# More x transposes on TensorE, earlier q and k transposes and a new step order in an attention and SwiGLU kernel

## The chip, the cores and the metric

The kernel runs on one core of one Trainium2 chip. The metric is the device time of that core in microseconds (us) for one execution. One execution of each kernel was also recorded by the hardware profiler; the page and the trace of a kernel come from that one execution, and the timed series has three to eleven executions.

## The reference

The reference computes attention in a sliding window and feeds it to a gated feed-forward block (FFN). Cut to what matters:

```python
# q, k, v: (8, 8, 576, 64) float32;  x: 4608 tokens of 512;  d_ff = 1536
scores = scale * np.matmul(q, k.transpose(0, 1, 3, 2))
mask = np.abs(pos[:, None] - pos[None, :]) <= 32
attn = softmax(np.where(mask, scores, -1e9))            # written out in the original
x = (attn @ v).transpose(0, 2, 1, 3).reshape(4608, 512)
g, val = x @ w_gate, x @ w_val
out = (g / (1 + np.exp(-g)) * val) @ w_out               # float32, 4608 x 512
```

## The kernel before

The tokens pass through the FFN in nine chunks of 512. Chunk 0 is done in a prologue. Each of the chunks 1 to 8 is a list of steps: two 128-wide units (u50, u51) and five groups of seven products (0P1 to 4P7, a Strassen-Winograd scheme in which x and weights are added before the products and sums are formed after), then FFN2 as seven larger products (F1 to F7). While FFN2 of one chunk runs, the attention of the next batch is woven in: score tiles (sc), exponentials (ex), masks (k), attention products (av) and norms (m, n). The letter after a slash is the engine of a step (D VectorE, G GpSimd, A ScalarE), and @ gives PSUM banks.

On each engine the steps stand in the order in which the program issues them. That holds for the queue of SyncE too, called SPq in the profile: it carries the output sends, the DMA transposes of x, q and k, and the shifts of v, each in program order, and a transfer that has to wait holds up all that stand behind it.

An FFN product needs x with the model dimension on partitions, so each pair of 64-token tiles has to be turned. Pairs that are "urgent" are turned on TensorE, the others by a DMA transpose:

```python
def turn_x(ms, pool, cast=None):
    ...
    if pool is None:
        nc.sync.dma_start_transpose(out=dst, in_=x16[0])
        return
    ...
    for n, x in enumerate(x16):
        for g in range(GS):
            nc.tensor.transpose(out=tp[:, n, g, :], in_=x[:, 128 * g:128 * g + 128],
                                identity=ident)
```

The q and k of a batch arrive as tokens through GpSimd's queue, one chunk ahead of their use, and are turned by DMA, five pieces of q and five of k per batch:

```python
def turn_qk(b, m):
    turn_tok(toks.pop(("q", b, m)), qT[b % 2], m, 0)
    turn_tok(toks.pop(("k", b, m)), kT[b % 2], m, 32)
```

And the part of the chunk that says when this happens, with two steps:

```python
URGENT = {1: (1, 2), 2: (1, 2), 3: (0, 1), 4: (1,), 5: (0,)}

def chunk(j, name, todo):
    b = j + 1
    if 2 < b < B:
        load_v(b, range(5))
    ...
    def norm_carried(i):
        pair_norm(pairs[i])
        pair_xt(pairs[i])                 # DMA transpose of the carried pair
        if i == len(pairs) - 1 and b < B:
            for m in range(5):
                turn_qk(b, m)             # ten transposes, all behind the norm
                if m == 3:
                    shift_v_dma(b)
    ...
    def norm(i):
        pair_norm(todo[i])
        if i not in urgent:
            pair_xt(todo[i])
```

"F6" is the third of FFN2's seven products to be issued, "Fc11" the addition that makes the first output block and sends it.

Of the kernel before, what the change touches and what calls it, by code (L numbers as in the profile page):

```python
# [132 lines left out]
def kernel(  # L133
# [12 lines left out]
    B, H, S, D = q.shape  # L146
# [647 lines left out]
    for u in range(FKS):  # L794
# [14 lines left out]
        if u == 10:  # L809
# [35 lines left out]

    ORDER = {
        "first": """
            u50g0@2 u50v0@3 T1/G av@4@5 u50g1 ld0 u50v1 T3/D n0 u50s T2/D u50m 0P1@1 W0 0s1 1P1@0 W1
            ld1 1s1 0P2@7 1P5@5 0P5@6 ld2 0c11 0P6 0p5 W2 1P6 T4/D ld3 1P2@3 2P1@4 0u2 1c11 0P7 0c22
            ld4 1p5 2P5@2 1u2 W3 0P3 1P7 ld5 2p5 0c12 2s1 1c22 1P3 0P4 2P6 3P1@7 0sc 0sd ld6 1c12 2u2  # L850
            W4 2P2@6 1P4 0hm ld7 3s1 2P7 ld8 1sc 2c22 3P6 1sd 3u2 4P1@3 2sc ld9 2P3 2c11 2P4 3P2@5
            1hm 3P5@1 2c12 3P7 4s1 3c11 S10/G S12/G S00/G S11/D 2sd 3p5 4P6 3c22 4P5@6 u51g0@0 S13/G
            u51g1 2hm S20/G S02/D 4u2 4P7 4p5 3P4 4c22 3sc 4P2@2 4P4 u51s 3sd S22/D 3P3 S01/D S03/G
            4P3 4c11 3c12 4sc 4sd u51v0@7 4c12 tabE S21/G 3hm 4h1 S30/G u51v1 4h0 u51m S31/D sc0@4@5
            sc12@0@1@2@3 S40/D ex0 F1a@6 F1 S50/D ex2 S41/D k2 Fs1 S51/G k0 F2@7 ex1 S42/G F6 k1 W5
            S32/G Fc11 av012@4@5@0@1@2@3 Fu2 m0 F5 Fk5 sc34@4@5 m1 ex3 m2 S52/G S43/G S53/G tabS
            S23/D S33/D F7 xtp@2@3 Fc22 F3 W6 xtc/A k3 F4 Fc21 Fc12
        """,
        "even": """
            u50v0@3 u50g0@2 T3/D av@4@5 T1/G u50g1 u50v1 n0 u50s u50m 1P1@6 T2/G 0P1@0 1P5@7 1s1  # L860
            1P2@4 0P2@1 1P6 ld0 0s1 1c11 0P5@5 2P1@3 0c11 0P6 1p5 ld1 1u2 0p5 1P7 3P1@2 0u2 2s1 1c22
            2P5@4 T4/D 0P7 1P3 3s1 0c22 1P4 1c12 0P3 ld2 1sc 1sd 0c12 0P4 0sc ld3 ld4 1hm 2P6 2P2@7
            3P2@1 0sd 3P6 ld5 2p5 4P1@0 0hm 2c11 2u2 3u2 ld6 2P7 4s1 3P5@6 3P7 3c11 S12/G 3p5 2c22
            4P6 3c22 2P3 2P4 2c12 4P5@5 S00/G 2sc 4u2 3P4 S10/D S02/G 2sd S11/D 4P7 4p5 2hm S01/G
            4c22 ld7 3P3 3c12 u51g0@1 3sd 3sc u51g1 4P4 ld8 3hm S32/D 4sc 4P2@6 S03/G 4P3 u51s S30/G
            4sd S20/D u51v0@7 4c11 u51v1 4c12 tabE S22/G u51m ld9 S31/D sc12@0@1@2@3 sc0@4@5 ex2 4h0
            ex0 S50/G 4h1 F1a@6 F1 S21/D S40/D S51/G S23/D k2 F2@7 S41/G Fs1 k0 ex1 k1 S52/G Fc11
            S33/D S13/D S42/D F6 av012@4@5@0@1@2@3 Fu2 F5 m0 S53/D m1 Fk5 m2 F7 sc34@4@5@0@1 S43/D
            ex4 xtp@2@3 F3 Fc22 xtc/D F4 ex3 k4 tabS Fc12 Fc21 k3
        """,  # L870
        "odd": """
            T3/D u50g0@2 u50v0@3 T1/G av@4@5@0@1 u50g1 T2/G n0 u50v1 ld0 u50s u50m n1 0P1@7 1P1@6
            T4/G 1P2@4 0P5@5 0s1 1P5@2 ld1 1s1 1P6 1u2 0P2@3 0P6 4P1@0 1p5 1P7 2P1@1 0u2 1P3 1c11
            0c11 1c22 0p5 1c12 0P7 1P4 2s1 2P6 1sc ld2 ld3 1sd 0c22 ld4 1hm ld5 0P3 2P5@4 0sc 3P1@3
            ld6 2u2 2P2@2 2p5 0c12 0P4 2P3 3s1 2c11 S10/D 4s1 2P7 3P6 3P5@6 0sd 4P6 3P2@5 S11/D 2c12
            2c22 3u2 S13/G 3P7 2P4 3p5 0hm 4u2 3c11 4P5@2 2sc 2sd 3c22 2hm 4P7 4p5 ld7 4c22 3P4 3sc
            S12/G ld8 3P3 u51g0@7 u51g1 3sd 3c12 4P4 3hm 4P3 4sc S00/D 4c12 4P2@6 4c11 u51v0@4 S22/G
            u51s u51v1 4sd u51m 4h0 S50/D 4h1 S51/D S02/G S30/D sc12@0@1@2@3 S20/G S40/D S31/D F1a@6
            tabE ex1 S01/G F1 S21/G ld9 k1 sc0@4@5 ex2 k2 Fs1 S32/D F2@7 S41/G ex0 F6 S33/G k0 Fc11
            S52/D S43/D S42/D Fu2 av012@4@5@0@1@2@3 F5 Fk5 S53/D S23/D S03/D m0 F7 sc34@4@5 m2 F3 m1  # L880
            Fc22 ex3 xtp@2@3 F4 k3 tabS xtc/D Fc21 Fc12
        """,
        "seven": """
            u50g0@2 u50v0@3 av@4@5@0@1 u50v1 u50g1 u50s n0 n1 T1/G u50m 1P1@6 0P1@7 2P1@5 1s1 0s1
# [20 lines left out]
    def table(func):  # L905
        nc.scalar.activation(out=dummy, in_=rall[0:1, 0, 0:1], func=func, bias=0.0, scale=1.0)

    URGENT = {1: (1, 2), 2: (1, 2), 3: (0, 1), 4: (1,), 5: (0,)}

    def chunk(j, name, todo):  # L910

        nonlocal one, two
        b = j + 1
        if 2 < b < B:
            load_v(b, range(5))
        hts[j] = htpool.tile([128, FKS, 512], FP16, tag="ht", name="hT")
        xs, xsteps = x_sums(j)
        pairs = list(carried)
        carried[:] = todo[3:]
        n = len(todo)  # L920
        urgent = URGENT.get(j, ())
        loads = [(m, c) for m in range(5) for c in "qk"] if b + 1 < B else []
        engines = {"P": nc.tensor, "A": cast_act, "D": nc.vector, "G": nc.gpsimd}
        ex, turned = {}, []

        def av(i, pool=None):
            if i < n:
                pair_av(todo[i], pool, False)

        def attention():  # L930
            for i, m in enumerate(pairs):
                pair_av(m, (two[2], two[0])[i], False)

        def norm_carried(i):
            pair_norm(pairs[i])
            pair_xt(pairs[i])
            if i == len(pairs) - 1 and b < B:
                for m in range(5):
                    turn_qk(b, m)
                    if m == 3:  # L940
                        shift_v_dma(b)

        def scores(ids):
            for i in ids:
                if i < n:
                    ex[i] = pair_scores(todo[i], two[(2, 0, 1, 2, 0)[i]], False)
# [6 lines that stand above are left out]
        def load():  # L953
            if loads:
                m, c = loads.pop(0)
                load_qk(b + 1, (m,), c)

        steps = {"av": attention, "sc0": lambda: scores((0,)), "sc12": lambda: scores((1, 2)),
                 "sc34": lambda: scores((3, 4)),
                 "av012": lambda: [av(i, two[(2, 0, 1)[i]]) for i in range(3)],  # L960
                 "tabE": lambda: table(AF.Exp), "tabS": lambda: table(AF.Silu),
                 "xtp": lambda: turned.append(turn_x([todo[i] for i in urgent], two[1]))
                 if urgent else None,
                 "xtc": lambda eng: turned.pop()(cast_act if eng is cast_act else cast_dve)
                 if urgent else None,
                 "check": lambda: good.append(check_range()), "flag": lambda: set_flag(good[0], one[5])}
        for i in range(2):
            steps[f"n{i}"] = lambda i=i: norm_carried(i)
        for i in range(5):
            steps[f"ex{i}"] = lambda i=i: ex[i]()  # L970
            steps[f"k{i}"] = lambda i=i: pair_mask(todo[i])
            steps[f"m{i}"] = lambda i=i: norm(i)
        for i in range(10):
            steps[f"ld{i}"] = load
        for i in range(7):
            steps[f"W{i}"] = tw[i + 1]
        steps.update(xsteps)
        for f in range(5):
            for s, fn in group_steps(j, f, xs).items():
                steps[f"{f}{s}"] = fn  # L980
        for c in range(2):
            for s, fn in unit_steps(j, FKS - 2 + c, None if c or j == NCH - 1 else two[1]).items():
                steps[f"u5{c}{s}"] = fn
        for p in range(6):
            for k in range(4):
                steps[f"S{p}{k}"] = lambda eng, p=p, k=k: wino_sum(j, p, k, eng)

        stage = 0 if two else 1
        for token in ORDER[name].split():
            step, _, eng = token.partition("/")  # L990
            step, *banks = step.split("@")
            if stage == 0 and banks and step[:3] != "av" and step[:3] != "u50":
                one, two = open_psum(*[(f"ps_{i}", 1) for i in range(8)]), None
                stage = 1
            elif stage == 1 and todo and step in ("sc0", "sc12", "F1a"):
                two = open_psum(*[(f"ps_{i}", 1) for i in ("01", "23", "45", "6", "7")])
                stage = 2
            if step == "F1a":
                steps.update(wino_steps(j, j == NCH - 1, one if j == NCH - 1 else
                                        two[3:] if todo else one[6:]))  # L1000
            if eng:
                steps[step](engines[eng])
            elif stage == 1 and banks and step[0] != "F":
                steps[step](one[int(banks[0])])
            else:
                steps[step]()
# [42 lines left out]
```

## Time and profile before

| Before | |
|---|---|
| time, median of 3 runs | 337.9 us (335.4 to 338.69) |
| the recorded execution | 333.11 us, its records span 331.4 us |
| mean granted TensorE clock in it | 0.988 |
| TensorE busy | 303.4 us, 92% of the span |
| idle of TensorE in chunks 1 to 6 | 13.7 us |

The lines that name the waits are shown in the prediction. Read them as follows: in the list of waits, the line before the arrow is what stood still and the one after it what it waited for, then the total, the number and the longest wait. In the table of stretches, each row is a part of the span, and after its length comes the busy time of TensorE, its weight loads, VectorE, ScalarE and GpSimd, each with its count in brackets, then the granted clock, the DMA share and GB/s.

One more table shows the surroundings of the x wait at the end of chunk 4, in the same columns:

```profile
197.12:199.25 2.13, 0.00 (x0) 0.00 (x1) 0.37 (x2) 1.01 (x3) 0.00 (x0) 1.00 1.64 155
199.25:200.27 1.02, 1.02 (x6) 0.36 (x8) 0.00 (x0) 0.00 (x0) 0.94 (x1) 1.00 1.09 385
200.27:203.68 3.41, 3.41 (x41) 2.06 (x41) 0.90 (x2) 0.53 (x1) 3.32 (x4) 0.50 0.37 106
```

TensorE does nothing for 2.13 us; a microsecond after it resumed, its clock is granted at 0.50 for 3.41 us.

### The profile page before, as it was taken

The numbers are of one execution on the slowest core, as the hardware profiler recorded it, in microseconds if no ns is written. First come the engines' busy times: TensorE is split into PE (matmuls) and PEld (weight loads), VectorE is DVE, ScalarE is ACT, GpSimd is POOL, SyncE is SP. The second block draws the span as 40 slices with busy tenths as digits, with TensorE's granted clock in tenths as the row PEclk, the third lists the DMA queues.
The fourth block names the chain that finished last, engine by engine and source line by source line (L and its number), as shares of the span: only waits on it lengthen the run. The fifth ranks groups of instructions, "written<-read, shape, count | busy, mean of one in ns | idle before, by whom it ended". The sixth has DMA issues, their size and how long they took to land. (4 is left out here: it accounts for less than half of the span.)

```text
span 331.4 us, 8641 instructions
## 1 busy us (share of the span) xinstructions
PE 303.4 (92%) x3380; PEld 230.5 (70%) x3380; DVE 260.6 (79%) x501; ACT 217.7 (66%) x358; POOL 194.3 (59%) x245
## 2 busy tenths in 40 slices
PE   5789999898899998998999879989999999999991
PEld 2444555585678676886788666868787778878880
DVE  3845997798978996798869984898699978956970
ACT  3864569587468945796489653984699369529720
POOL 8972786926896683968576839477243333330440
PEclk9999999999999999999999997999999999999997
DMA  7999999999199999999999999999954250030012
GB/s 279 175 210 303 220 162 191 175 138 149 34 182 138 157 103 189 107 150 136 163 161 156 102 136 148 152 164 109 176 103 91 65 144 3 0 128 2 2 57 80
DMA packets 155920, 44.26 MB, mean 134 GB/s; under 512 B 136416, under 2 KB 153312, under 8 KB 155872
## 3 DMA queue, kind: packets, MB, share of 16 engines
q0 software_dynamic: 100640, 16.52, 71.6%
q1 hardware_dynamic: 55232, 27.11, 42.0%
q8 instruction: 28, 0.46, 0.6%
q14 instruction: 20, 0.16, 0.2%
HBM read 37.75 MB, written 9.44 MB: 142 GB/s over the span
## 5 line engine op out<-in xcount | busy, mean ns | idle before, releaser
L624 POOL TENSOR_TENSOR s_top<-hT 128x256 f16<-128x256 f16 x48 | 37.6, 800 | 57.2 <-DVE hT L535 42.7
L273 ACT ACTIVATE kept<-gX_ps 128x512 f32<-128x512 f32 x80 | 45.7, 598 | 11.5 <-PE gX_ps L509 9.2
L329 ACT ACTIVATE p_t<-s_ps 128x1024 f16<-128x1024 f32 (+1 forms) x40 | 35.8, 935 | 7.8 <-PE s_ps L323 7.6
L509 PEld LDWEIGHTS <-wv 128*128 128x128 f16 x320 | 31.6, 99 | 7.7 <-issue 2.6
L535 DVE TENSOR_TENSOR hT<-silu,val 128x1024 f16<-128x1024 f16 (+1 forms) x48 | 34.1, 724 | 1.2 <-ACT silu L531 0.4
L526 DVE TENSOR_TENSOR gate<-gX_ps,kept 128x512 f32<-128x512 f32 x40 | 27.5, 687 | 8.7 <-ACT kept L273 5.1
L521 DVE TENSOR_TENSOR val<-gY_ps,kept 128x512 f16<-128x512 f32 x40 | 26.9, 685 | 8.2 <-PE gY_ps L509 7.8
L653 PEld LDWEIGHTS <-s_top 128*128 128x128 f16 x288 | 27.3, 98 | 5.2 <-issue 0.8
L653 PEld LDWEIGHTS <-hT 128*128 128x128 f16 x288 | 27.1, 98 | 5.0 <-DVE hT L535 0.9
L509 PEld LDWEIGHTS <-g_top 128*128 128x128 f16 x288 | 28.2, 98 | 3.3
L228 POOL DMA_DIRECT2D tok<-in_k_dram x30 | 25.9, 864 | 7.2 <-DMA qT<-tok 6.8
L333 DVE TENSOR_TENSOR p_t<-p_t,mask 128x1024 f16<-128x1024 f16 x32 | 26.1, 843 | 4.3 <-ACT p_t L329 4.2
L509 PE MATMUL gX_ps<-x_sums,g_top 128*128 128x256 f16 x192 | 28.0, 273 | 0.0
L521 DVE TENSOR_TENSOR val<-gZ_ps,kept 128x512 f16<-128x512 f32 x40 | 27.2, 684 | 0.9 <-PE gZ_ps L509 0.4
L531 ACT ACTIVATE silu<-gate 128x512 f16<-128x512 f32 x40 | 25.1, 629 | 3.4 <-DVE gate L526 3.3
L509 PEld LDWEIGHTS <-g_more 128*128 128x128 f16 x256 | 25.1, 98 | 3.3
L228 POOL DMA_DIRECT2D tok<-in_q_dram x30 | 26.0, 867 | 1.9 <-DMA kT<-tok 1.1
L273 ACT ACTIVATE kept<-gZ_ps 128x512 f32<-128x512 f32 x40 | 23.9, 598 | 3.1 <-PE gZ_ps L509 2.9
L403 DVE TENSOR_TENSOR x<-o_ps,rall 128x512 f16<-128x512 f32 x36 | 24.9, 692 | 1.2
L531 ACT ACTIVATE silu<-gX_ps 128x512 f16<-128x512 f32 x40 | 23.9, 598 | 2.9 <-PE gX_ps L509 2.3
L509 PE MATMUL gX_ps<-x_sums,wg 128*128 128x256 f16 x160 | 24.0, 272 | 1.6 <-DVE gate L526 1.6
L624 POOL TENSOR_TENSOR s_top<-s_top,hT 128x256 f16<-128x256 f16 x23 | 18.9, 828 | 9.4 <-DVE s_top L624 9.1
(122 smaller groups left out, 689.8 us busy)
## 6 DMA issues: line engine op xcount, KB each, us to landing
out_dram<-osb SPq DMA_DIRECT2D x32, 256.0 KB, 3.9
v<-v SPq DMA_DIRECT2D x12, 264.0 KB, 5.6
v<-in_v_dram POOLq DMA_DIRECT2D x24, 128.0 KB, 5.7
tok<-in_q_dram POOLq DMA_DIRECT2D x24, 128.0 KB, 6.8
tok<-in_k_dram POOLq DMA_DIRECT2D x24, 128.0 KB, 6.7
qk_st<-in_q_dram SPq DMA_DIRECT2D x4, 576.0 KB, 7.0
qk_st<-in_k_dram SPq DMA_DIRECT2D x4, 576.0 KB, 8.8
v<-in_v_dram POOLq DMA_DIRECT2D x16, 96.0 KB, 5.4
```

Source lines behind the costliest of these rows:

```text
L228: nc.gpsimd.dma_start(out=t[0:n].rearrange("p (h d) -> p h d", d=D), in_=src[b].rearrange("h s d -> s h d")[128 * m:128 * m + n])
L273: nc.scalar.activation(out=o, in_=i, func=AF.Copy, bias=0.0, scale=1.0)
L329: nc.scalar.activation(out=o, in_=s, func=AF.Exp, bias=0.0, scale=1.0 / float(D) ** 0.5)
L333: nc.vector.tensor_tensor(out=flat, in0=flat, in1=mask, op=ALU.mult)
L403: nc.vector.tensor_tensor(out=x16s[m][:, a], in0=ov[:, :, :, 0:D], in1=r.unsqueeze(3).to_broadcast([128, a.stop - a.start, 4, D]), op=ALU. ...
L509: nc.tensor.matmul(out=k[name][:, n], lhsT=lhs[:, g, 128 * n:128 * n + 128], rhs=rhs[:, g, :], start=(pool is not None and n == 0 and g == 0),
L521: nc.vector.tensor_tensor(out=k["val"][:, :, cols(c)], in0=k[src], in1=k[name], op=ALU.add)
L526: nc.vector.tensor_tensor(out=k["gate"], in0=k["X"], in1=k["p5"], op=ALU.add)
L531: nc.scalar.activation(out=k["silu"][:, :, cols(c)], in_=k[src], func=AF.Silu, bias=0.0, scale=1.0)
L535: nc.vector.tensor_tensor(out=hts[j][:, 2 * f:2 * f + 2, c], in0=k["silu"][:, :, c], in1=k["val"][:, :, c], op=ALU.mult)
L624: eng.tensor_tensor(out=o, in0=a, in1=b, op=op)
L653: nc.tensor.matmul(out=dst[n], lhsT=lhs[:, f, 128 * n:128 * n + 128], rhs=rhs[:, f, :], start=(first and f == 0 and (split or n == 0)), st ...
```

## The change

The intent: all x that the next chunk needs at once is turned on TensorE, so that no DMA has to land in time; the q and k transposes start earlier, from FFN2 of the chunk before; and the order of steps in chunks 1 to 6 is replaced by one that is meant to tolerate small shifts. It has three parts, which I call X, T and O.

```diff
     ORDER = {
         "first": """   ... 10 lines replaced (part O) ...
         "even": """
 ... (the FFN2 part of it)
-            4sd S20/D u51v0@7 4c11 u51v1 4c12 tabE S22/G u51m ld9 S31/D sc12@0@1@2@3 sc0@4@5 ex2 4h0
-            ex0 S50/G 4h1 F1a@6 F1 S21/D S40/D S51/G S23/D k2 F2@7 S41/G Fs1 k0 ex1 k1 S52/G Fc11
-            S33/D S13/D S42/D F6 av012@4@5@0@1@2@3 Fu2 F5 m0 S53/D m1 Fk5 m2 F7 sc34@4@5@0@1 S43/D
-            ex4 xtp@2@3 F3 Fc22 xtc/D F4 ex3 k4 tabS Fc12 Fc21 k3
+            S11/G S21/D S30/G u51v1 4sd 4c11 tabE 4c12 u51m 4h0 4h1 sc12@0@1@2@3 S23/G ex1 F1a@6 ex2
+            S50/D S32/G S31/G S40/D F1 sc0@4@5 k1 S02/D F2@7 S41/G Fs1 ex0 k2 S13/D S51/G S52/D k0
+            S33/D F6 Fc11 av012@4@5@0@1@2@3 S43/D Fu2 S42/D m0 F5 m1 F7 m2 sc34@4@5@0@1 xtp@2@3 S03/D
+            Fk5 S53/D ex4 Fc22 F3 ex3 xtc/D tabS F4 k4 Fc12 k3 Fc21
         "odd": """     ... 10 lines replaced ...
-    URGENT = {1: (1, 2), 2: (1, 2), 3: (0, 1), 4: (1,), 5: (0,)}          # part X
+    URGENT = {1: (0, 1, 2), 2: (0, 1, 2), 3: (0, 1), 4: (0, 1), 5: (0,)}
+    turned_ahead = set()                                                  # part T, to the end
 ... in chunk(), at its top:
+        if b < B:
+            for m in range(4):
+                if (b, m) not in turned_ahead:
+                    turn_qk(b, m)
+            shift_v_dma(b)
 ... in norm_carried():
-                for m in range(5):
-                    turn_qk(b, m)
-                    if m == 3:
-                        shift_v_dma(b)
+                turn_qk(b, 4)
 ... in the loop over the steps:
+            if step == "F6" and b + 1 < B:
+                for m in range(2):
+                    turn_qk(b + 1, m)
+                    turned_ahead.add((b + 1, m))
```

In the old "even" order and in the new "odd" order, F6 stands behind Fc11, so that the early transposes of part T stand behind the first output's send in the queue. In the other new orders, F6 stands ahead of Fc11, and they stand ahead of the send. The x that the kernel before waits for is that of chunks 3 and 5, sent at the ends of chunks 2 and 4, which have the "even" order.

More of the change, by code (lines that the diff above doesn't have):

```diff
@@ L847 @@
         "first": """
-            u50g0@2 u50v0@3 T1/G av@4@5 u50g1 ld0 u50v1 T3/D n0 u50s T2/D u50m 0P1@1 W0 0s1 1P1@0 W1
-            ld1 1s1 0P2@7 1P5@5 0P5@6 ld2 0c11 0P6 0p5 W2 1P6 T4/D ld3 1P2@3 2P1@4 0u2 1c11 0P7 0c22
-            ld4 1p5 2P5@2 1u2 W3 0P3 1P7 ld5 2p5 0c12 2s1 1c22 1P3 0P4 2P6 3P1@7 0sc 0sd ld6 1c12 2u2
-            W4 2P2@6 1P4 0hm ld7 3s1 2P7 ld8 1sc 2c22 3P6 1sd 3u2 4P1@3 2sc ld9 2P3 2c11 2P4 3P2@5
-            1hm 3P5@1 2c12 3P7 4s1 3c11 S10/G S12/G S00/G S11/D 2sd 3p5 4P6 3c22 4P5@6 u51g0@0 S13/G
@@ L853 @@
-            u51g1 2hm S20/G S02/D 4u2 4P7 4p5 3P4 4c22 3sc 4P2@2 4P4 u51s 3sd S22/D 3P3 S01/D S03/G
-            4P3 4c11 3c12 4sc 4sd u51v0@7 4c12 tabE S21/G 3hm 4h1 S30/G u51v1 4h0 u51m S31/D sc0@4@5
-            sc12@0@1@2@3 S40/D ex0 F1a@6 F1 S50/D ex2 S41/D k2 Fs1 S51/G k0 F2@7 ex1 S42/G F6 k1 W5
-            S32/G Fc11 av012@4@5@0@1@2@3 Fu2 m0 F5 Fk5 sc34@4@5 m1 ex3 m2 S52/G S43/G S53/G tabS
-            S23/D S33/D F7 xtp@2@3 Fc22 F3 W6 xtc/A k3 F4 Fc21 Fc12
+            W0 W1 u50v0@3 u50g0@2 u50g1 av@4@5 u50v1 T1/G n0 u50s T2/D u50m 1P1@7 ld0 1P2@1 0P1@6
@@ new lines @@
+            0P5@0 1s1 T3/D 1P5@4 ld1 ld2 0s1 1P6 ld3 0P6 1u2 1c11 0P2@5 2P1@2 1p5 T4/D 1P7 W2 0c11
+            1P3 0u2 2s1 0P7 2P5@1 ld4 1c22 1c12 0p5 W3 1sc ld5 0P3 2p5 1P4 2P6 3P1@3 2P2@4 0c22 0P4
+            1sd 4P1@5 2u2 0sc 0c12 1hm 3s1 2P7 3P6 W4 2P3 S12/D 2c11 0sd 4s1 0hm 3u2 3P5@0 2c22 3P2@7
+            3P7 S00/D 4P6 2P4 ld6 ld7 3p5 2c12 3c22 3c11 2sc S01/G 4u2 4P5@1 3P4 2sd 4P7 3P3 S10/G
+            u51g0@4 2hm S20/G 4p5 3sc u51g1 4c22 3sd 3c12 4P4 3hm 4P3 S11/D 4P2@6 4sc S21/G u51v0@7
@@ L858 @@
+            S30/G 4c12 u51s 4c11 S03/G u51v1 u51m 4sd 4h0 sc0@4@5 ld8 sc12@0@1@2@3 tabE F1a@6 ld9 ex0
+            4h1 S23/D S50/D S40/D ex2 F1 S31/G Fs1 S51/D k0 F2@7 ex1 k2 S41/G S22/D F6 k1 Fc11 S52/G
+            av012@4@5@0@1@2@3 S32/G F5 S53/D S33/D S13/G m0 Fu2 sc34@4@5 S02/G m2 S42/G m1 Fk5 S43/D
+            ex3 W5 tabS F7 xtp@2@3 xtc/A Fc22 F3 W6 F4 k3 Fc12 Fc21
         """,
         "even": """
-            u50v0@3 u50g0@2 T3/D av@4@5 T1/G u50g1 u50v1 n0 u50s u50m 1P1@6 T2/G 0P1@0 1P5@7 1s1
@@ L861 @@
-            1P2@4 0P2@1 1P6 ld0 0s1 1c11 0P5@5 2P1@3 0c11 0P6 1p5 ld1 1u2 0p5 1P7 3P1@2 0u2 2s1 1c22
-            2P5@4 T4/D 0P7 1P3 3s1 0c22 1P4 1c12 0P3 ld2 1sc 1sd 0c12 0P4 0sc ld3 ld4 1hm 2P6 2P2@7
-            3P2@1 0sd 3P6 ld5 2p5 4P1@0 0hm 2c11 2u2 3u2 ld6 2P7 4s1 3P5@6 3P7 3c11 S12/G 3p5 2c22
-            4P6 3c22 2P3 2P4 2c12 4P5@5 S00/G 2sc 4u2 3P4 S10/D S02/G 2sd S11/D 4P7 4p5 2hm S01/G
-            4c22 ld7 3P3 3c12 u51g0@1 3sd 3sc u51g1 4P4 ld8 3hm S32/D 4sc 4P2@6 S03/G 4P3 u51s S30/G
@@ L866 @@
-            4sd S20/D u51v0@7 4c11 u51v1 4c12 tabE S22/G u51m ld9 S31/D sc12@0@1@2@3 sc0@4@5 ex2 4h0
-            ex0 S50/G 4h1 F1a@6 F1 S21/D S40/D S51/G S23/D k2 F2@7 S41/G Fs1 k0 ex1 k1 S52/G Fc11
-            S33/D S13/D S42/D F6 av012@4@5@0@1@2@3 Fu2 F5 m0 S53/D m1 Fk5 m2 F7 sc34@4@5@0@1 S43/D
-            ex4 xtp@2@3 F3 Fc22 xtc/D F4 ex3 k4 tabS Fc12 Fc21 k3
+            u50g0@2 u50v0@3 u50g1 T1/G av@4@5 u50v1 u50s n0 u50m 0P1@7 T2/G T3/G 1P1@0 0P5@1 1P2@6
+            1s1 1P5@4 0s1 0p5 1P6 1c11 0P2@5 0c11 1u2 0P6 1p5 3P1@2 1P7 0P3 ld0 0u2 ld1 T4/D 1c22
@@ new lines @@
+            2P1@3 0P7 0c12 2P5@6 1P4 1P3 ld2 2s1 2P6 1sc 4P1@5 0c22 2P2@1 ld3 0P4 0sc ld4 1c12 1sd
+            2u2 ld5 2P7 2p5 3s1 ld6 4s1 2P3 1hm 3P6 0sd 2c11 ld7 3u2 S10/D 2c22 4P6 2c12 2sc 0hm
+            3P5@0 3P2@4 3P7 2P4 3c11 3p5 4u2 3c22 4P5@6 2sd ld8 S00/G 4P7 3P4 4p5 S01/D 3sc 3P3 2hm
+            3sd 4c22 4sc u51g0@1 u51g1 S12/G 3c12 4P4 S20/G 4P2@7 4P3 u51v0@4 S22/D ld9 u51s 3hm
+            S11/G S21/D S30/G u51v1 4sd 4c11 tabE 4c12 u51m 4h0 4h1 sc12@0@1@2@3 S23/G ex1 F1a@6 ex2
+            S50/D S32/G S31/G S40/D F1 sc0@4@5 k1 S02/D F2@7 S41/G Fs1 ex0 k2 S13/D S51/G S52/D k0
@@ L870 @@
+            S33/D F6 Fc11 av012@4@5@0@1@2@3 S43/D Fu2 S42/D m0 F5 m1 F7 m2 sc34@4@5@0@1 xtp@2@3 S03/D
+            Fk5 S53/D ex4 Fc22 F3 ex3 xtc/D tabS F4 k4 Fc12 k3 Fc21
         """,
         "odd": """
-            T3/D u50g0@2 u50v0@3 T1/G av@4@5@0@1 u50g1 T2/G n0 u50v1 ld0 u50s u50m n1 0P1@7 1P1@6
-            T4/G 1P2@4 0P5@5 0s1 1P5@2 ld1 1s1 1P6 1u2 0P2@3 0P6 4P1@0 1p5 1P7 2P1@1 0u2 1P3 1c11
-            0c11 1c22 0p5 1c12 0P7 1P4 2s1 2P6 1sc ld2 ld3 1sd 0c22 ld4 1hm ld5 0P3 2P5@4 0sc 3P1@3
@@ L875 @@
-            ld6 2u2 2P2@2 2p5 0c12 0P4 2P3 3s1 2c11 S10/D 4s1 2P7 3P6 3P5@6 0sd 4P6 3P2@5 S11/D 2c12
-            2c22 3u2 S13/G 3P7 2P4 3p5 0hm 4u2 3c11 4P5@2 2sc 2sd 3c22 2hm 4P7 4p5 ld7 4c22 3P4 3sc
-            S12/G ld8 3P3 u51g0@7 u51g1 3sd 3c12 4P4 3hm 4P3 4sc S00/D 4c12 4P2@6 4c11 u51v0@4 S22/G
-            u51s u51v1 4sd u51m 4h0 S50/D 4h1 S51/D S02/G S30/D sc12@0@1@2@3 S20/G S40/D S31/D F1a@6
-            tabE ex1 S01/G F1 S21/G ld9 k1 sc0@4@5 ex2 k2 Fs1 S32/D F2@7 S41/G ex0 F6 S33/G k0 Fc11
@@ L880 @@
-            S52/D S43/D S42/D Fu2 av012@4@5@0@1@2@3 F5 Fk5 S53/D S23/D S03/D m0 F7 sc34@4@5 m2 F3 m1
-            Fc22 ex3 xtp@2@3 F4 k3 tabS xtc/D Fc21 Fc12
+            u50g0@2 T3/G T1/G u50v0@3 av@4@5@0@1 T2/G u50v1 ld0 n0 u50g1 u50s ld1 n1 u50m 0P1@7 0s1
+            0P2@6 1P5@4 1P1@0 ld2 ld3 1s1 0P6 2P1@3 0c11 1P2@6 0P5@5 1p5 T4/D 0u2 0p5 1P6 0P7 1u2
+            1c11 2P2@1 0c22 0P3 2s1 0c12 1P7 0sc 1c22 ld4 0P4 2P5@2 1P3 0sd 2P6 3P1@7 0hm 2p5 1sc 2u2
+            3s1 4P1@6 1P4 2P7 3P6 ld5 2P3 1c12 2c11 2c22 1sd 4s1 1hm 3P5@5 3u2 S00/G 4P6 3P7 S10/D
@@ new lines @@
+            2c12 S02/G S01/G 3p5 3P2@4 S12/G 2P4 2sc S03/G 4P5@1 3c22 4u2 3c11 2sd 4P7 ld6 3P4 S11/D
+            2hm 4p5 3P3 4c22 3sc u51g0@2 u51g1 ld7 4P4 4P2@0 3c12 3sd 3hm 4P3 u51v0@7 4sc S20/G ld8
+            S13/D 4c11 u51s 4c12 S30/D 4sd u51v1 4h1 tabE S21/G 4h0 S22/G u51m S40/D sc0@4@5 S50/D
+            ld9 sc12@0@1@2@3 S31/G F1a@6 F1 ex0 ex1 F2@7 Fs1 S51/G k0 S41/D k1 S43/D ex2 S23/D k2
+            Fc11 S42/D F6 S32/D S53/G av012@4@5@0@1@2@3 S52/D F5 m0 m1 sc34@4@5 Fu2 Fk5 S33/D m2 F7
@@ L882 @@
+            F3 xtp@2@3 ex3 tabS Fc22 k3 Fc12 F4 xtc/D Fc21
         """,
```

## The prediction

> **What bounds the kernel now.** I read the busy shares first, then TensorE's own list of waits, then stretches cut at the chunk borders, and last the timeline around the longest waits.
>
> ```profile
> PE 303.4 (92%) x3380; PEld 230.5 (70%) x3380; DVE 260.6 (79%) x501; ACT 217.7 (66%) x358; POOL 194.3 (59%) x245
> DMA  7999999999199999999999999999954250030012
> ```
>
> TensorE is busy 92% of 331.4 us, so it is the bound and can gain at most its idle 28 us. The row of digits says that the DMA engines are over 90% busy in nearly every slice of the first three quarters: a transfer there waits its turn. The list of TensorE's waits (total, times, longest) names who holds it up:
>
> ```profile
> PE gv_ps L583 <- DMA xT<-x: 3.6, 2, 2.1
> PE o_ps L385 <- DVE p_t L333: 2.7, 8, 0.6
> PE s_ps L323 <- DMA kT<-tok: 2.0, 2, 1.1
> PE gX_ps L509 <- DVE gate L526: 1.6, 2, 0.9
> PE s_ps L323 <- DVE val L521: 1.5, 3, 0.5
> PE gX_ps L509 <- DVE hT L594: 1.4, 1, 1.4
> PE y_ps L653 <- DVE osb L682: 0.8, 1, 0.8
> ```
>
> No single cause leads; it is a dozen short waits. Cut at the starts of chunks 1 to 6, the only ones whose order changes (the orders "seven" and "last" are the same text), the stretches are (window, length, busy of each engine, clock, DMA share, GB/s):
>
> ```profile
> 58.60:95.20 36.60, 32.29 (x378) 25.80 (x377) 31.91 (x59) 24.54 (x40) 25.02 (x31) 1.00 1.29 123
> 95.20:130.40 35.20, 32.50 (x395) 26.06 (x393) 29.71 (x56) 24.97 (x41) 22.43 (x28) 1.00 1.70 154
> 130.40:163.60 33.20, 32.18 (x393) 26.17 (x394) 27.55 (x57) 22.90 (x38) 24.55 (x28) 1.00 1.52 140
> 163.60:199.25 35.65, 32.24 (x390) 25.79 (x388) 29.99 (x57) 24.97 (x41) 22.70 (x28) 1.00 1.50 144
> 199.25:233.50 34.25, 33.15 (x388) 26.59 (x389) 26.83 (x57) 22.87 (x38) 24.33 (x28) 0.95 1.46 142
> 233.50:266.30 32.80, 31.65 (x387) 25.75 (x386) 28.32 (x53) 23.57 (x39) 11.92 (x15) 1.00 0.48 107
> ```
>
> Length less PE busy is the idle time: 4.3, 2.7, 1.0, 3.4, 1.1 and 1.2, together 13.7 us. This is all that the change can touch; prologue and last two chunks stay. In the timeline, the two largest kinds look so:
>
> ```profile
> 149.59 2.55 SPq L234 DMA_TRANSPOSE qT<-tok  x1
> 151.84 0.29 PE L323 MATMUL s_ps<-qT,kT 64*128 64x64 f16 x8 [0.90 <-DMA kT<-tok]
> 152.23 1.19 SPq L234 DMA_TRANSPOSE kT<-tok  x1
> 192.18 3.19 SPq L419 DMA_TRANSPOSE xT<-x  x2
> 199.25 0.61 PE L583 MATMUL gv_ps<-xT,wg 128*128 128x512 f16 x2 [2.13 <-DMA xT<-x]
> ```
>
> In odd chunks the ten q and k transposes, issued only after the carried pair's norm, are still in the queue when the scores need them. And x sent to DMA at 192.2 is first usable at 199.25, 7 us later, although the next chunk's first product needs it.
>
> **What the skill says.** "VectorE: DVE Perf Modes", section "The three transpose paths", gives 390 ns for a 128x128 transpose on TensorE and 1309 ns on the DMA path. The trace agrees in direction, but in chains: four on TensorE take 0.39 to 0.40 us together, eight 0.61; one x transpose (four blocks) by DMA holds its queue 1.2 us and lands after 4.6 us in the median. "DMA: Bandwidth & Descriptors", section "Issuing engines are not separate DMA queues", says transfers issued by different engines share the same 16 DMA engines and interleave. The 90% digits and the 7 us agree. "Perfetto Trace Analysis", section "Optimizing Scalar/DVE Operations", says that GpSimd and VectorE share an SBUF read port. It shows: an x sum on VectorE took 1.38 us beside GpSimd's at 58.3 us, against a usual 0.42; so who takes which sum matters. No page bears on the step order itself.
>
> **The change part by part.** The built programs differ by 12 TensorE transposes with their 12 weight loads; counts of products, exponentials and sums stay.
>
> (1) x turned on TensorE. Chunks 1, 2 and 4 turn one pair more, each with four matmuls. Two of these pairs are the ones awaited at 130.4 (1.43 us) and 199.25 (2.13 us). Removed: 3.56. Added on TensorE: eight against four costs 0.21, so 3 x 0.21 = 0.6. The evacuating copies grow by a pair too (0.41 to 0.69 on VectorE; 0.60 to 1.00 to 1.47 on ScalarE), but one or two FFN2 products of 1.3 us lie between transposes and the next chunk, so I count them as hidden. Net gain 2.9.
>
> (2) q and k transposes early. Four of ten now stand before the FFN2 sums' sends in the queue's program order, four at the chunk's top, two after the carried norm. One holds the queue 1.2 to 2.5 us, so four fewer after the norm end the series 5 us or more earlier, against waits of 0.90 and 1.10 (plus 0.1 of the same kind). Gain 2.0. They also free token buffers earlier; the wait of GpSimd for those (5 us once) has no cost on TensorE in the list.
>
> (3) The order. I followed each wait to its producer in both programs.
> - Chunk 1, first product: today it waits 1.41 for VectorE's hT of unit 50. The new first product goes to a bank that the last prologue eviction freed, and only the second waits for hT: four matmuls cover 0.43. VectorE has three w_top (0.55 each) ahead of it instead of one and the 1.38 sum: 1.65 against 1.93, another 0.28. Gain 0.7.
> - Chunk 1, gate waits (0.77 and 0.87): VectorE stood 1.38 us for a GpSimd sum that directly preceded its use. Now four VectorE steps, some 2.8 us, lie between that sum and its use. Gain 1.4.
> - Chunk 1, the second y product waits 0.84 for the first output's addition, which stood behind a 1.02 us weight sum. That moves away. Gain 0.7.
> - Even chunks: the first attention product waits 0.73 each time for the last mask (3 x 0.73 = 2.2), and the last score tile 0.53, 0.53 and 0.40 for a VectorE addition. The new order gives that tile's bank later and puts a sum and two products around it; but now the first FFN2 product waits for the same addition, with only the 0.87 us of two score tiles and unit 51 before it. I give it half: 1.8.
>
> Sum of (3): 4.6. All three: 2.9 + 2.0 + 4.6 = 9.5 us of the 13.7.
>
> **Less new waits.** Every order puts something new on an edge. I take 0.4 us for each of the six reordered chunks, 2.4 in all, an estimate from the size of the small waits in the list (0.2 to 0.6). Net: 9.5 - 2.4 = 7.1, so 337.9 - 7.1 = 330.8 us, 2.1% less.
>
> **Rivals.**
> First, a wait takes the place of the one removed. VectorE is busy 26.8 to 31.9 us in stretches of 33 to 37: when TensorE closes up, VectorE has less time for the same work. In odd chunks the k wait of 1 us now lets VectorE catch up before FFN2; without it FFN2's first product may wait for hT instead. For: the same chain (addition, hT, product) already costs 0.5 in even chunks. Against: odd chunks have 2 us less VectorE work than even ones. Then (2) gives nothing and (3) half: 2.9 + 2.3 - 1 = 4.2, or 333.7.
>
> Second, the early transposes collide. They enter a DMA system that is already full, beside token and v loads, and in odd chunks stand in the queue between the first output's send and the second's, where four of them need 5 to 6 us. An output buffer returning late would stop VectorE or ScalarE, and the v loads could land late. For: the 90% digits. Against: the work is the same, only moved, and outputs of the next chunk's gates come over 5 us later. It would eat (2) and some of (1): 334 to 335.
>
> Third, the gain is larger than the trace shows. The unprofiled runs took 335.4 to 338.7, the profiled 333.1. If the extra 2 to 6 us are waits that vary from run to run, an order with slack wins part of them too: 327. If they are clock throttling (two stretches of half clock in this trace, 0.988 in the mean), nothing is won. The trace can't tell.
>
> **Range and chances.** Between the second rival (335) and the third (327) lies my range: 327 to 335. The limit of 2% is 331.1, which is practically my point value: the chance of more than 2% faster is 0.50, within 2% 0.47. Slower than 344.7 would need new waits of over 16 us in six chunks: 0.03.
>
> **What would show it.** If right: TensorE's list has no wait on xT<-x and none on kT<-tok; L425 has 76 matmuls instead of 64; chunk 1 loses about 3 us, chunks 2 and 4 about 2 to 3 each, chunks 3 and 5 about 1; idle time in chunks 1 to 6 falls from 13.7 to about 6. If the first rival: waits on hT L535, val L521 or p_t L333 grow in the odd chunks. If the second: VectorE or ScalarE waiting for DMA on osb, or attention products waiting for v. The prediction is wrong if PE idle in chunks 1 to 6 falls by under 4 or over 11 us, or if the time moves without it, through the clock.

## The result and the profile after

The changed kernel takes 324.86 us in the median of 4 runs (324.24 to 325.4); the kernel before, with one more run beside it, takes 337.98 us (335.4 to 338.69). The ratio is 0.9624, with a 95% interval of 0.9571 to 0.9678, so it is 3.8% faster. Ratios here are the mean time of one kernel's fast runs over that of the other's in the same rounds, so they are not quite the ratio of the medians that I quote. On one core a run counts as slow if it is over 1.5% above the fastest of its kernel, and in the sessions of the experiments, one to four of the eleven widely spread runs of the kernel before are left out by that rule.

The time lies below my range (327 to 335), while the direction was right.

From the page of the changed kernel, first the busy shares, then the clock by slices:

```profile
PE 301.0 (93%) x3392; PEld 230.6 (71%) x3392; DVE 257.0 (80%) x498; ACT 217.0 (67%) x358; POOL 195.7 (61%) x248
PEclk9999999999999999999999999999999999999997
```

TensorE has twelve instructions more and is busy 2.4 us less: the row of the clock has no slice below 9 before the last, so the half-clock stretch within the kernel is gone. The list of TensorE's waits, same columns as before:

```profile
PE o_ps L385 <- DVE p_t L333: 3.8, 6, 1.5
...
PE gY_ps L509 <- DVE hT L594: 1.0, 1, 1.0
PE s_ps L323 <- DVE val L521: 0.7, 2, 0.4
```

In this list no line says xT<-x and none says kT<-tok: TensorE waits for no DMA in the reordered chunks. The waits for x (3.6 us) and for k (2.0 us) are not shortened, they are absent. One is new: attention products now wait 1.5 us for a mask in chunk 1. The stretches, cut at the starts of chunks 1 to 6:

```profile
59.26:93.88 34.62, 31.84 (x382) 26.11 (x381) 31.64 (x59) 24.64 (x40) 23.79 (x30) 1.00 1.40 143
93.88:126.98 33.10, 32.16 (x399) 26.23 (x397) 28.14 (x55) 24.01 (x39) 23.93 (x29) 1.00 1.60 153
126.98:159.80 32.82, 31.96 (x395) 26.31 (x393) 28.90 (x56) 23.63 (x41) 24.33 (x30) 1.00 1.41 126
159.80:192.96 33.16, 32.10 (x394) 26.02 (x392) 28.06 (x55) 23.90 (x39) 25.67 (x31) 1.00 1.84 165
192.96:225.54 32.58, 31.74 (x390) 26.09 (x388) 28.36 (x56) 23.79 (x41) 22.94 (x28) 1.00 1.52 133
225.54:258.27 32.73, 31.96 (x386) 25.42 (x384) 26.51 (x53) 23.20 (x39) 11.85 (x15) 1.00 0.71 111
```

The six lengths sum to 199.0 us against 207.7 before, 8.7 less. Length less busy time gives an idle of 7.3 us against 13.7, 6.4 less; the other 2.3 us are busy time that went away, 1.7 of it the half-clock stretch shown above. Chunk by chunk the trace lost 2.0, 2.1, 0.4, 2.5, 1.7 and 0.1 us. Prologue and the last two chunks changed by 0.7 us at most.

How the border from chunk 2 to chunk 3 looks now, in the timeline (start, duration, engine, line, operation):

```profile
109.36 1.84 SPq L234 DMA_TRANSPOSE kT<-tok  x1
...
123.68 0.84 PE L425 MATMUL xt_ps<-ident,x 128*128 128x128 f16 x12
...
126.98 0.59 PE L583 MATMUL gv_ps<-xT,wg 128*128 128x512 f16 x2
```

Three pairs are turned on TensorE in 0.84 us; the next chunk's first product starts with no wait in brackets behind it. And a k transpose for the scores of chunk 3 already runs at 109 us in chunk 2, before any output of this chunk is sent.

So, from one recorded execution to the other, the span fell from 331.4 to 323.1 us, by 8.3, which is near my 7.1. But the medians differ by 13.1. The recorded execution of the kernel before was 4.8 us below the median of its runs; that of the changed kernel (324.83 us) sits at its median. The experiments had to explain this second amount.

### The profile page after: what moved, and what is told of

Same layout as the page of the kernel before. It is cut to its first block, busy times and chain, and to the rows that moved or that the text cites. A ratio compares the mean times of both kernels' runs of the same rounds, so it can differ in the third digit from the quotient of the medians.

```text
span 323.1 us, 8668 instructions
## 1 busy us (share of the span) xinstructions
PE 301.0 (93%) x3392; PEld 230.6 (71%) x3392; DVE 257.0 (80%) x498; ACT 217.0 (67%) x358; POOL 195.7 (61%) x248
## 5 line engine op out<-in xcount | busy, mean ns | idle before, releaser
L624 POOL TENSOR_TENSOR s_top<-hT 128x256 f16<-128x256 f16 x43 | 30.7, 722 | 60.6 <-DVE hT L535 42.5
L535 DVE TENSOR_TENSOR hT<-silu,val 128x1024 f16<-128x1024 f16 (+1 forms) x48 | 32.8, 695 | 1.9 <-ACT silu L531 1.2
L624 POOL TENSOR_TENSOR s_top<-s_top,hT 128x256 f16<-128x256 f16 x30 | 23.9, 802 | 14.8 <-DVE s_top L624 8.5
L565 POOL TENSOR_TENSOR x_sums<-xT 128x512 f16<-128x512 f16 x12 | 15.2, 1270 | 22.3 <-DVE xT L276 14.2
```

What stands on the lines that cost most here:

```text
L535: nc.vector.tensor_tensor(out=hts[j][:, 2 * f:2 * f + 2, c], in0=k["silu"][:, :, c], in1=k["val"][:, :, c], op=ALU.mult)
L624: eng.tensor_tensor(out=o, in0=a, in1=b, op=op)
```

## The experiments

The theory: the waits for x and for the q and k transposes are waits for DMA that are longer in most executions than in the one recorded, and the change takes them away with whatever they had beyond the trace. The rivals: the half clock is the cost and leaves for some other reason; or one part alone does all, for instance the order. In each session the kernel before ran beside the others on the same chip.

### The kernel before, once more (before_again)

No edit.

> The kernel before, unchanged, to see how its runs differ from one another. Theory T (a late x costs twice: TensorE idles, and the half clock that follows costs 1.7 us more per 3.4 us stretch): ratio 1.00; runs from 333 to 339 us, and the slower ones show a lower granted clock, about 0.005 per 1.7 us; the new profile has half-clock stretches right after the waits on xT<-x at the starts of chunks 3 and 5. Rival R (the runs differ by waits of VectorE and PSUM alone): the clock of all runs is the same within 0.002, and the differences sit in waits of TensorE on VectorE.

Measured: 335.88 us (334.42 to 337.74), ratio to its own runs as "before" 0.9994 [0.9951, 1.0038]. With these runs differences over half a per cent can be told apart; in the later experiments the interval is up to 0.8% on each side. The granted clock ranged from 0.979 to 0.992 and the recorded execution had 4.4 us of x waits against 3.6 in the first, so the waits do differ between executions of one program. Of the two half-clock stretches that I had expected after the x waits, one came, at the start of chunk 3; the other stood in chunk 5 after a wait of 1.0 us for k.

### Part X alone, on the old order (x_only)

```diff
-    URGENT = {1: (1, 2), 2: (1, 2), 3: (0, 1), 4: (1,), 5: (0,)}
+    URGENT = {1: (0, 1, 2), 2: (0, 1, 2), 3: (0, 1), 4: (0, 1), 5: (0,)}
```

> Only the x part on the old order. Theory T: the two waits on xT<-x are gone and with them the half-clock stretches, so 5 to 8 us less than before, 330 to 333 us, clock 0.992 or more, runs within 1 us of each other. Rival R: the gain is the two waits of the trace less the added transposes, 3 us, 335 us, and the spread of the runs stays.

Measured: 328.76 us (327.75 to 330.62) beside 336.94, ratio 0.9794 [0.9749, 0.9838]. One line of the diff gives 7 to 8 us, more than twice the 2.9 that I had put on it, and a little beyond theory T's 330 to 333 us; the runs lie 2.9 us apart and not within 1. TensorE waits for no x, and its waits for k stay as they were:

```profile
PE s_ps L323 <- DMA kT<-tok: 2.1, 3, 1.3
```

### Part T alone, on the old order (qk_only)

```diff
 (part T as in the change; URGENT and ORDER as before)
```

> Only the early q and k transposes on the old order. Theory T: the waits on kT<-tok go (2.0 us), the waits on xT<-x stay or grow because the x transposes now share the queue with four more transposes: 335 to 338 us, still spread. Rival R: 2 us less, 336 us.

Measured: 340.36 us (339.64 to 343.17), ratio 1.0128 [1.0091, 1.0164]: it is slower, by about 4 us. The waits for k are gone, but TensorE now waits far longer for x:

```profile
PE gv_ps L583 <- DMA xT<-x: 9.8, 2, 5.4
```

The queue of SyncE at the end of chunk 2 shows why:

```profile
124.76 0.39 SPq L668 DMA_DIRECT2D out_dram<-osb  x1
125.26 1.33 SPq L234 DMA_TRANSPOSE qT<-tok  x1
...
131.19 1.52 SPq L419 DMA_TRANSPOSE xT<-x  x1
```

In the old "even" order, F6 stands behind Fc11, so that the four early transposes stand behind the first output's send and ahead of the x transpose of the next chunk. The queue starts x at 131.19; in the kernel before, it did at 123.80 (shown below). What was meant to relieve k delays x by 7 us. The end of chunk 4 looks the same. In chunk 1 of the same execution, where F6 stands ahead of Fc11, the four had started by 86.60, ahead of the send at 89.89; x followed at 90.74, and TensorE did not wait for it. (The recorded execution, 343.17 us, is the slowest of the seven.)

### Part T on the old order, one step earlier (qk_early_F2)

```diff
-            if step == "F6" and b + 1 < B:
+            if step == "F2" and b + 1 < B:          # part T alone otherwise
```

F2 stands ahead of Fc11 in every order, so the four transposes now stand ahead of the first send in chunks 2 and 4 too.

> As the run with only the q and k part on the old order, which was 4.3 us slower than before, but the four early transposes are issued from the step F2, which stands before the first output's send in every chunk, instead of F6, which in the old order stands behind it. Theory Q (the loss was x queueing behind four transposes that themselves stood behind the send): they now run well ahead, the waits on xT<-x fall from 9.8 us to 2 to 4, those on kT<-tok stay away, and the time is 2 to 4 us under before, 333 to 335 us, ratio 0.988 to 0.994. Rival (the early transposes crowd the DMA engines at any place): 339 us or more, as before this edit.

Measured: 331.57 us (330.35 to 332.0), ratio 0.991 [0.9834, 0.9986]; the runs of the kernel before on the same chip spread from 332.4 to 339.2 us. That is about 9 us less than part T with its trigger at F6 in the other session, for one word of difference. All early transposes have run by 115.5 us, and x gets the queue directly after the send:

```profile
121.25 0.39 SPq L668 DMA_DIRECT2D out_dram<-osb  x1
122.70 2.00 SPq L419 DMA_TRANSPOSE xT<-x  x1
```

So it is the place in the queue, not the DMA work, that made part T costly. With it in the right place, part T alone wins 3 to 5 us (by the ratio or by the medians), although TensorE still waits 4.9 us for x in two places.

### Parts X and T on the old order (x_qk_old_order)

```diff
 (parts X and T as in the change; ORDER as before)
```

> Both DMA parts on the old order: all of the change but the order. Theory T: about 7 to 9 us less, 329 to 331 us, tight runs; the order is left with 4 to 6 us. Rival R: 5 us less, 333 us, and the order is left with 8.

Measured: 326.98 us (326.64 to 328.0), ratio 0.9734 [0.9697, 0.9771]. TensorE waits for no DMA in the chunks. In chunks 2 and 4 the early transposes still stand behind the first send, but the x that was awaited is no longer behind them: it isn't in the queue. The same part T that cost 4 us alone gains about 2 on top of X.

### The new order alone (order_only)

```diff
 (the three ORDER strings of the change; URGENT and turn_qk as before)
```

> Only the new step order. Theory T (waits on x cost twice; the order itself is worth some 2 us, as the step from both DMA parts to the whole change was): 334 to 336 us, ratio 0.993 to 0.997, still with waits on xT<-x and half-clock stretches, clock 0.980 to 0.988. Rival S (the order is worth the 4.6 us of the prediction by itself): 332.5 us, ratio 0.986.

Measured: 330.64 us (329.28 to 333.3) beside 336.52, ratio 0.983 [0.9764, 0.9897]. I had expected 334 to 336, from the small step between x_qk_old_order and the changed kernel, and missed; the rival's 332.5 was nearer. The waits for x (4.0 us) and k (0.7 us) are still there in part, so the order does not work by removing them all.

### The new order with X, and with T (order_x, order_qk)

```diff
 (order_x:  parts O and X)
 (order_qk: parts O and T)
```

> New order and x on TensorE, q and k transposes late as before. Theory T: no half-clock stretch, waits on kT<-tok of 1 us each or more in chunks 3 and 5 and perhaps in others: 326 to 328 us, ratio 0.967 to 0.973. Rival S: the order's slack hides these waits too, 325 us.

> New order and early q and k transposes, but x of the first pair still by DMA. Theory T: in the new order of even chunks the four early transposes stand before the first output's send and are issued well ahead, so x does not queue behind them as it did with the old order; the waits on xT<-x return at 2 us each with their half clock: 330 to 333 us, clock 0.982 to 0.990. Rival (early transposes delay x in any order): 338 us or more, as with the old order.

Measured: order_x 327.1 us (324.65 to 327.56), ratio 0.9682 [0.9617, 0.9746], with 0.5 us of waiting for k left. order_qk 328.72 us (326.65 to 331.81), ratio 0.97 [0.9627, 0.9772], with 5.2 us of waiting for x in three places. On the new order part T gains 1.9 us over the order alone by the medians of the same session (four runs each, which spread over 4 and 5 us), where on the old order it lost 4: F6 now stands ahead of the first send in chunks 2 and 4, whose x is the one awaited. The rival that early transposes delay x in any order had 338 us or more. In order_x I had expected waits for k of 1 us or more, and found one of 0.5.

### Filling the x wait with idle products (fill_before)

If the half clock after the x wait is what costs, keeping TensorE busy through that wait should win its 1.7 us. The kernel before got nine products without use at the start of chunks 3 and 5, as long as the wait (2.1 us).

```diff
+        if j in (3, 5):
+            warm = two[1].tile([128, 512], FP32, tag="b", name="warm")
+            mf = mask.rearrange("p a q -> p (a q)")
+            for _ in range(9):
+                nc.tensor.matmul(out=warm, lhsT=mf[:, 0:128], rhs=mf[:, 0:512], start=True, stop=True)
```

> The kernel before with nine dummy products (some 1.9 us of TensorE) at the tops of chunks 3 and 5, where it waits for x. They give no result and remove no wait. Theory T: TensorE's idle there falls under 0.5 us, the half-clock stretches go, clock 0.991 or more, 2 to 3 us less than before: 334 us, ratio 0.990 to 0.994. Rival C (the half clock has another cause, such as time or heat, and the late x costs only its wait): the same time or 0.5 us more, clock 0.980 to 0.988 as before.

Measured: 337.89 us (335.24 to 340.58), ratio 1.0033 [0.9974, 1.0091]: no gain. One execution with a mean clock of 0.997 still took 336.7 us. The list of waits shows where the time went:

```profile
PE s_ps L323 <- DMA kT<-tok: 4.5, 3, 2.0
...
PE gv_ps L583 <- DMA xT<-x: 0.4, 1, 0.4
```

The wait for x was filled and the one for k grew from 2.0 to 4.5 us. Both are on one chain: x lands, the first product and, behind it on TensorE, the carried pair's attention products run, its norm follows, only then the ten q and k transposes enter the queue, and the scores wait for the last. With a late x the whole chain is late, however TensorE spends the time. But the half clock was not kept away: the recorded execution has a stretch of 3.41 us in chunk 5 after two waits for k, and five of the six executions have clocks of 0.982 to 0.988, as the kernel before has. So the run shows that time won at the x wait is lost again at the k wait; what a half clock costs it does not decide, and the clock behaved as the run's rival had said.

### Two more looks at the kernel before (before_look2, before_look3)

No edit; one recorded execution each, to see what a slower execution of the same program has in it.

> One more profile of the kernel before. Theory: if this execution takes 336 us or more, then against the first profile (333.1 us) its extra time lies in longer or more waits on xT<-x and kT<-tok and in half clock after them, in chunks 2 to 5, and chunks 6 to 8 are the same within 0.3 us. Rival: the extra is spread over all chunks, or over the prologue.

> As the look before it: another profile of the kernel before, to see where a slower execution is slower.

Measured: 333.68 us with a clock of 0.988, and 337.1 us with 0.986. The second is the slower kind that the median describes. First its waits for x, then the x transpose of chunk 3 and the product that waits for it, then its chunks 2 and 3:

```profile
PE gv_ps L583 <- DMA xT<-x: 5.3, 2, 3.3
```

```profile
123.66 1.21 SPq L419 DMA_TRANSPOSE xT<-x  x1
...
132.15 1.03 PE L583 MATMUL gv_ps<-xT,wg 128*128 128x512 f16 x2 [3.33 <-DMA xT<-x]
```

```profile
95.07:132.15 37.08, 32.48 (x395) 26.02 (x392) 28.86 (x55) 24.95 (x41) 22.74 (x28) 0.99 1.60 158
132.15:167.77 35.62, 34.68 (x393) 26.99 (x394) 27.40 (x57) 22.77 (x38) 26.22 (x28) 0.92 1.19 114
```

Against the first recorded execution (35.20 and 33.20 us), chunk 2 is 1.9 us longer and chunk 3 2.4. Its chunks 6 to 8 are the same within 0.2 us. The 1.9 us are the longer wait. The 2.4 us are half clock: TensorE is busy 34.68 us in chunk 3 against 32.18 for the same work, its idle time is the same, and the clock is 0.92. It was at half for 6.8 us, from the last microsecond of the wait of 3.3 us on. And the cause of that wait is not a late start. This is the queue in the first recorded execution of the kernel before:

```profile
123.80 1.21 SPq L419 DMA_TRANSPOSE xT<-x  x1
```

There, x was usable at 130.4 us, 6.6 us later. In the slower execution the transpose was issued at 123.66 us and usable at 132.15, 8.5 us later. The same transfer, issued at the same time within 0.14 us, landed 1.9 us later. That is shown; why it did is not: the records do not tell what the DMA engines did for it.

Over the four recorded executions of the kernel before, chunks 1 to 5 took on average 1.7, 2.9, 1.2, 2.6 and 1.7 us more than in the changed kernel, and chunks 6 to 8 nothing. Nearly all that varies between them, and all that the change won, lies in the same chunks.

### The change with one part taken out (after_ref, less_order, less_x)

```diff
 (after_ref:  the changed kernel)
 (less_order: the changed kernel with the ORDER strings of before)
 (less_x:     the changed kernel with the URGENT of before)
```

> The changed kernel once more, as the yardstick for the three runs beside it on one chip, since the earlier ones came from several chips and from rounds whose kernel before differed. Ratio 0.962 to 0.970, 324 to 326 us, spread under 2 us.

> The changed kernel with the old order. If the order's share on top of the others is what its waits in the traces say (2.2 us from 325.3 to 323.1), 2 to 2.5 us over the changed kernel; if the ratios of the separate rounds are right, 3.7 us over.

> The changed kernel without the x part. By the waits on xT<-x of its first profile (5.2 us in three places) less the 0.6 us of transposes saved: 4 to 5 us over the changed kernel, spread over 4 us; by the separate ratios 2.6 us over.

Measured in one session, the kernel before at 337.41 us:

| Kernel | median us (lowest to highest) | ratio, interval | the part is worth |
|---|---|---|---|
| after_ref | 324.69 (323.31 to 325.32) | 0.9637 [0.9599, 0.9676] | |
| less_order | 327.74 (326.9 to 329.1) | 0.9723 [0.9686, 0.9761] | O: 3.0 us |
| less_x | 329.41 (326.14 to 333.73) | 0.977 [0.9715, 0.9826] | X: 4.7 us |

For T, order_x is the changed kernel without it: 327.1 us, in another session, so about 2 us. As last parts put in, the three give some 10 us, of about 13. Alone on the old kernel X gives 7 to 8 us and O 5.7, and T loses 4. They do not add. That each removes waits on the same chain is my reading; no run isolates it.

less_x came out as the waits in the trace of order_qk had said (4 to 5 us, spread over 4), less_order between its two expectations (2 to 2.5 and 3.7).

The spread says more than the medians. Without X, the six runs lie 7.6 us apart; with it, 2.0. In the recorded execution of less_x TensorE waits 3.2 us for x in three places:

```profile
PE gv_ps L583 <- DMA xT<-x: 3.2, 3, 2.0
```

The kernel before is spread too (332.4 to 341.0 us over all sessions), the changed kernel is not (323.3 to 325.4 in two sessions). It is no rule, though: the four runs of qk_early_F2 wait for x by DMA and lie within 1.7 us.

### Trying to beat both (mended, mend_first)

The largest wait that is new is that of the attention products for a mask in chunk 1. Two variants of the changed kernel give those masks earlier; the first also turns the order of the attention products in the even chunks.

```diff
 (both, chunk 1; mend_first also has "Fs1 k0 S51/D" and "Fc11 S22/D S52/G")
-  ... ld0 1P2@1 0P1@6
-  4h1 S23/D S50/D S40/D ex2 F1 S31/G Fs1 S51/D k0 F2@7 ex1 k2 S41/G S22/D F6 k1 Fc11 S52/G
+  ... ld0 0P1@6 1P2@1
+  4h1 S23/D S50/D S40/D ex1 F1 S31/G Fs1 S51/D k0 F2@7 ex2 k1 S41/G S22/D F6 k2 Fc11 S52/G
 (mended only, even chunks)
-  S33/D F6 Fc11 av012@4@5@0@1@2@3 S43/D Fu2 S42/D m0 F5 m1 F7 m2 ...
+  S33/D F6 Fc11 av120@4@5@0@1@2@3 S43/D Fu2 S42/D m1 F5 m2 F7 m0 ...
```

> The changed kernel with its three largest remaining waits of the reordered chunks attacked by order alone: in chunk 1 the mask of the second attention product is made before the third's (wait of 1.54 us), one more product is put ahead of the one that waits for hT (1.01 us), and in even chunks the attention products run in the order 1, 2, 0 as their masks are ready (0.5 us three times). Theory: each wait on TensorE in these places is path: 2 to 3 us less than the changed kernel, ratio 0.953 to 0.957, 322 us. Rival: new waits eat half: 1 us less, ratio 0.96.

> The changed kernel with only chunk 1 mended: one more product before the one that waits for hT, the masks in the order of the products, and a VectorE sum that the next product does not need moved behind the masks. The even chunks stay, since turning their product order round had only moved their waits. Theory: 1.3 us less than the changed kernel in the profile (0.45 and 0.9), 0.996 of its time; rival: the freed time is taken up by a later wait on VectorE in the same chunk, no difference over 0.3 us.

Measured: mended 325.16 us (324.05 to 326.68), ratio 0.9729 [0.9673, 0.9785]; mend_first 324.57 us (322.61 to 326.17), ratio 0.9637 [0.9587, 0.9687], the same as the changed kernel in its session. (The ratio of mended is against a session in which the kernel before had some faster runs; its median is within 0.5 us of that of the changed kernel.) No gain. In mended the mask wait fell from 3.8 to 2.0 us, and others took its place:

```profile
PE o_ps L385 <- DVE p_t L333: 2.0, 3, 1.3
PE y_ps L653 <- DVE osb L682: 1.5, 6, 0.4
```

In the timeline of mend_first, the scores of chunk 1 stand as long for the norm as the attention products had stood for the mask:

```profile
87.14 0.41 PE L323 MATMUL s_ps<-qT,kT 64*128 64x64 f16 x16 [0.96 <-DVE x L403]
```

All of these are VectorE's work, and VectorE is busy 31.6 of the 34.6 us of chunk 1. These two variants only changed which of its steps TensorE waits for. Whether it would wait less with work taken from VectorE was not tried. The changed kernel stays the best of those that ran.

## Why the prediction was wrong

**The mechanism held.** What I had said would show it does: no wait on xT<-x, none on kT<-tok, 76 transposes at L425, idle in chunks 1 to 6 at 7.3 us where I had said about 6. The idle time was not all that the change could touch, though, as I had said: 2.3 us of busy time went too. Chunks 2 and 4 lost what I had said (2.1 and 2.5), chunk 1 less (2.0 against 3), chunks 3 and 5 0.4 and 1.7 against 1. Of the first rival's waits in the odd chunks only two of 0.36 and 0.35 us came. The 2.4 us that I had set aside for new waits were about right: these two, 1.5 for the mask in chunk 1 and 0.6 for sums of GpSimd make 2.8.

**The step that failed** is "337.9 - 7.1 = 330.8". The 7.1 us were read from a recorded execution of 333.1 us and subtracted from a median that lay 4.8 us above it. This assumes that the 4.8 stay. They did not: in a slower execution they are the same waits, longer, and half clock beside them. The experiments show it in three ways: a slower execution has its extra time in chunks 2 and 3, 1.9 us of a later landing x and 2.4 of half clock (before_look3); a kernel that differs only in X gains 7 to 8 us, twice what its waits in the trace add up to; and the changed kernel's runs lie 2.0 us apart, but 7.6 when X alone is undone (less_x). The record adds a fourth: of the 44 executions of the kernel before that were timed beside the experiments, the four with a clock of 0.992 or more took 332.4 to 334.4 us, the fourteen with 0.983 or less 336.3 to 341.0. Had I subtracted the 8.3 us of the traces from 333.1, I would have had 324.8; with my own 7.1 it would have been 326.0.

**The third rival was the right one**, and I put it at the edge of the range (327) instead of near the middle. One of its sentences was wrong: "If they are clock throttling, nothing is won." The half-clock stretches went with the waits. Apart from the wait for the mask at the start of every execution, seven of the thirteen waits of 2 us or more of TensorE in the recorded executions, over all kernels, had a stretch at half clock beside them, and the changed kernel has no such wait and no such stretch. The clock is still not the main part, by an estimate: the recorded clocks average 0.986 over the 44 executions of the kernel before and 0.994 over ten of the changed kernel, which is some 3 us of the 13.

**Terms by their size.** X: 2.9 said, 4.7 measured on top of the rest and 7 to 8 alone. I had summed its two waits of 1.43 and 2.13 us from one execution, and counted nothing for the half clock beside them. An estimate from the records closes most of the gap: the four recorded executions of the kernel before wait 4.3 us for x on average, the clock of x_only (0.994 against 0.986 in its session) is worth 2.9 us, and the added transposes cost 0.6, which makes 6.6. That three DMA transposes fewer also let other transfers land sooner was not tested; the waits for k in x_only show no sign of it. T: 2.0 said and about 2 measured on top of the rest, but on the old order it lost 4 alone. That is a collision, as the second rival had said, but with x in the queue and not with output buffers or the loads of v. I had seen that in the new odd chunks four transposes stand between the sends; I had not seen that behind a send they hold up an awaited x, nor that X removes that transfer. O: 4.6 less 2.4, so 2.2 said, 3.0 measured on top and 5.7 alone.

**Within O**, by the recorded execution: in chunk 1 the gate waits went (1.6 us; 1.4 said), the y wait went (0.8; 0.7 said), and the first product's wait for hT fell by 0.4 (0.7 said). In the even chunks the attention products wait 0.5 instead of 0.7 us, and the last score tile's waits of 0.53, 0.53 and 0.40 us are gone, 2.1 us together where I had given 1.8. These are readings of one execution and of a size that its variation reaches.

**What stays open.** Why the same DMA transpose lands 1.9 us later in one execution than in another. What decides whether a shorter wait is followed by a half clock: some stretches stood after smaller waits, one after 1.0 us. And whether the recorded execution tends to be a fast one: in the 14 experiments with a series it was the fastest of its series in 6, where chance would give about 2.6, and the slowest in 2.

For the waits of 2 us or more the traces say more than I had read. All changes of the clock within the kernels lie on a grid of 3.413 us counted from the first clock record (57 steps, 194.56 us, to the stretch in the first recorded execution of the kernel before). Counted by the steps of this grid, TensorE was idle for 2.13 us or more of a step nine times before the last few us of a kernel, and half clock followed every time. The six long waits without a stretch lie across a border of the grid, with at most 1.75 us in one step. Of the 36 steps with 1.35 to 1.75 us of idle time, five were followed by half clock, so below 2 us this measure does not decide.

## What to carry to other kernels

Before a saving read from one trace is subtracted from a median, check that the recorded execution is as long as the median; if it is shorter and the waits in it are waits for DMA, look for the missing time in those same waits and in the half clock beside them. An x that the next stage needs at once is worth TensorE's 0.2 us per pair, since it takes out a transfer whose landing varies by microseconds. And when a transfer is moved earlier, look at its place in the queue, not only at its time: here, ahead of a send that waits for a result, part T alone gained 3 to 5 us, and behind it it lost 4.

## What the Trainium skill lacked or had wrong

- "DMA: Bandwidth & Descriptors" says in its section "Issuing engines are not separate DMA queues" that issuing engines share the 16 DMA engines. It gives no landing time for a transpose from SBUF to SBUF while these are loaded: here an x transpose of four blocks, 1.2 us long in its queue, took 3.7 to 7.0 us to land in the first recorded execution up to 240 us (5.3 in the median), where most digits of the DMA row are 9, 2.4 to 3.4 after that, where they fall, and 8.5 for one of them in another execution.
- No page that I read gives a cost for the place of a transfer in the issuing queue, before or after a send that waits: with the trigger at F6 the kernel took 340.4 us, at F2 331.6.
- "TensorE: Matmul & The Clock Gate", section "What's actually happening", states that the clock falls to half after one or more idle windows of about 3.4 us. The length agrees: the stretches at half clock within the kernels were 3.41 or 6.8 us. That section's threshold does not cover what the runs show: 2.13 us of idle time in one step of the 3.41 us grid were enough, and all nine steps with that much or more were followed by half clock. And a gap before the products is no measure of the gain: in fill_before it was filled and the ratio was 1.0033, since the DMA chain went on to hold TensorE elsewhere.
- No page that I read warns that the one recorded execution can be 4.8 us faster than the median of the same kernel (333.1 against 337.9).
